# Mish feed-forward on one core: the first w1 loads split, tile 0 transposed k by k, and b1 moved to SP's queue

## The chip, the cores and the metric

The kernel runs on one core of one Trainium2 chip. A core has a matrix engine (TensorE, in the profile PE, with its weight loads as PEld), a vector engine (DVE), a scalar engine for activation functions (ACT), a general engine (POOL) and a fifth sequencer (SP) that mostly issues DMAs. All of them run side by side, each on its own list of instructions, and meet only at semaphores. Sixteen DMA engines move data between device memory (HBM) and the on-chip memory (SBUF). Matmul results land in eight banks of PSUM.

The metric is the device time of one execution in microseconds, the median of several runs. Less is better.

## The reference

x is 2048 x 512 (bf16), w1 is 512 x 1792, b1 has 1792 values, w2 is 1792 x 512. What must be computed:

```python
h   = jnp.einsum("bsd,df->bsf", x, w1) + b1
sp  = jnp.log1p(jnp.exp(-jnp.abs(h))) + jnp.where(h > 0, h, 0)
act = h * jnp.tanh(sp)            # mish
out = jnp.einsum("bsf,fd->bsd", act, w2)
```

So there are two products with an activation between them: 2048 x 512 x 1792 and 2048 x 1792 x 512.

## The kernel before

The rows of x are worked in four blocks of 512 rows. For each block the first product is made transposed: for each of the 14 column groups f of w1 (128 columns each) four matmuls over k (the 512 inner values in groups of 128) gather h for 128 columns x 512 rows in one PSUM bank (`mm1`). ScalarE then writes mish of it, with the bias, to SBUF (`mish`, L153). The second product goes by tiles of 128 rows: 14 matmuls over f into a bank (`mm2`), which VectorE copies out (`put`, L192) and SP stores.

The first product needs x transposed, with k along the partitions. For blocks 1 to 3 the DMA engines do that while they load (`DMA_TRANSPOSE`, the last three loads on SP's queue). Block 0 would come too late that way, so its four 128-row tiles are loaded as they are and transposed on TensorE by `transpose_x` (L133 to L148): per tile four 128 x 128 transposes (one for each k) into PSUM, and two copies to SBUF, each of two k: VectorE takes k 0 and 1, ScalarE k 2 and 3.

Everything is written out by hand, so each engine works in the order of the program. The loads are issued on two queues (L91 to L112):

- on ScalarE's queue: w1 k 0-1 and w1 k 2-3, each for the first four column groups (256 KB each), then b1;
- on SP's queue: x tile 0, x tile 1 (128 KB each), x tiles 2 and 3 together (256 KB), w1 for column groups 4 to 7, w1 for groups 8 to 13, all of w2, then the three transposing loads.

While the first loads are under way TensorE runs six dummy matmuls of 512 columns (`WARM`, `dummy`). Then, with `first(js, ks)` standing for the products of tiles js with w1 rows ks for the first four column groups, its order is (L204 to L230):

```python
transpose_x(0); transpose_x(1)
first((0,), (0, 1)); first((1,), (0, 1)); first((0, 1), (2,))
transpose_x(2); transpose_x(3)
first((0, 1), (3,)); first((2, 3), (0, 1))
# b1: copied into a padded tile, transposed on TensorE, copied to b1_sb
first((2, 3), (2, 3))
```

A product of one tile has 128 moving columns, one of two tiles 256. After this come the ten remaining column groups of block 0 with 512 columns each, the second product of block 0, and the other three blocks. A matmul waits for the w1 load that it reads (`t_w1`) and for the copies of its tiles (`t_cp`), a transpose for the load of its tile (`t_xn`) and for the copy that last read its PSUM bank (`free`).

Of the kernel before, what the change touches and what calls it, by code (L numbers as in the profile page):

```python
# [4 lines left out]

P = 128
WARM = (512,) * 6
BLOCKS = (512, 512, 512, 512)


# [21 lines left out]
def bass_standalone__dense_activation_mish__prompt_kernel(  # L32
# [10 lines left out]
    BF, F32 = dt.bfloat16, dt.float32  # L43
# [3 lines left out]
    KT, FT = D // P, F // P  # L47
# [5 lines left out]
    F0 = 4  # L53
    N0 = BLOCKS[0] // P

    with ExitStack() as es:
        def sb(name, shape, t):
            return es.enter_context(nc.sbuf_tensor(name, shape, t))

        x_nat = sb("x_nat", [P, N0, D], BF)  # L60
        xT = sb("xT", [P, KT, S], BF)
        w1_sb = sb("w1_sb", [P, KT, F], BF)
        w2_sb = sb("w2_sb", [P, FT, D], BF)
        b1_nat = sb("b1_nat", [FT, P], BF)
# [6 lines left out]
        ps = es.enter_context(nc.psum_tensor("ps", [P, 8, 512], F32))  # L71

        def sem(name):
            return es.enter_context(nc.semaphore(name))

        sp = Stream(nc.sync, None)
        pe = Stream(nc.tensor, sem("c_pe"))
        dve = Stream(nc.vector, sem("c_dve"))
        act = Stream(nc.scalar, sem("c_act"))
        pool = Stream(nc.gpsimd, sem("c_pool"))  # L80

        def load(q, dst, src, name, transpose=False):
            s = sem(name)
            (q.eng.dma_start_transpose if transpose else q.eng.dma_start)(dst, src).then_inc(s, 16)  # L84
            return (s, 16)

        def load_w1(q, ks, a, b):
            return load(q, w1_sb[:, ks, a * P:b * P], w1v[:, ks, a * P:b * P], "s_w1_%d_%d" % (ks.start, a))


        t_xn, t_w1, t_w2 = [None] * N0, {}, {}  # L91
        for ks in (slice(0, 2), slice(2, 4)):
            t = load_w1(act, ks, 0, F0)
            for f in range(F0):
                for k in range(ks.start, ks.stop):
                    t_w1[k, f] = t
        for j in range(2):
            t_xn[j] = load(sp, x_nat[:, j, :], x2[j * P:(j + 1) * P, :], "s_xn%d" % j)
        t_xn[2] = t_xn[3] = load(sp, x_nat[:, 2:4, :], x2[2 * P:4 * P, :].rearrange("(j p) d -> p j d", p=P), "s_xn2")
        t_b1 = load(act, b1_nat[:, :], b1.rearrange("(j p) -> j p", p=P), "s_b1")  # L100
        for a, b in ((4, 8), (8, FT)):
            t = load_w1(sp, slice(0, KT), a, b)
            for f in range(a, b):
                for k in range(KT):
                    t_w1[k, f] = t
        t = load(sp, w2_sb[:, :, :], w2v, "s_w2")
        for f in range(FT):
            t_w2[f] = t
# [16 lines left out]
        def dummy(n):  # L125
            nc.tensor.matmul(ps[:, 7, 0:n], c_w, c_m[:, 0:n], start=True, stop=True)  # L126


        free = [[] for _ in range(8)]
        t_cp = {}  # L130
        t_mish = {}

        def transpose_x(j):  # L133

            pe.wait(t_xn[j], t_id)
            for h, eng in ((0, dve), (1, act)):
                bank = 2 * (j % 2) + h
                pe.wait(*free[bank])
                psb = ps[:, bank, 0:P].bitcast(BF)
                for i in range(2):  # L140
                    k = 2 * h + i
                    mm = nc.tensor.transpose(psb[:, i * P:(i + 1) * P], x_nat[:, j, k * P:(k + 1) * P], ident[:, :])  # L142
                eng.wait(pe.mark(mm))
                dst = xT[:, 2 * h:2 * h + 2, j * P:(j + 1) * P]
                src = psb.rearrange("p (k t) -> p k t", k=2)
                t = eng.mark(nc.vector.tensor_copy(dst, src) if eng is dve else act.eng.activation(dst, src, ACT.Copy))  # L146
                t_cp[j, h] = t
                free[bank] = [t]  # L148

        def mish(s, f, bank, t_mm):  # L150
            n = BLOCKS[s]
            act.wait(t_b1c, t_mm)
            t = act.mark(act.eng.activation(a_sb[:, f, starts[s]:starts[s + 1]], ps[:, bank, 0:n], ACT.Mish,  # L153
                                            bias=b1_sb[:, f:f + 1]))
            t_mish[s, f] = t
            free[bank] = [t]

        def mm1_step(s, f, k, bank, js=None):

            n = BLOCKS[s]  # L160
            lo, hi = (0, n) if js is None else (js[0] * P, (js[-1] + 1) * P)
            first = k == 0 and lo == 0
            if first:
                pe.wait(*free[bank])
            pe.wait(t_w1[k, f])
            if s:
                pe.wait(t_xT[s])
            else:
                pe.wait(*[t_cp[j, k // 2] for j in (js or range(N0))])
            return nc.tensor.matmul(ps[:, bank, lo:hi], w1_sb[:, k, f * P:(f + 1) * P],  # L170
                                    xT[:, k, starts[s] + lo:starts[s] + hi], start=first, stop=(k == KT - 1 and hi == n))

        def mm1(s, f, bank):
            for k in range(KT):
                mm = mm1_step(s, f, k, bank)
            mish(s, f, bank, pe.mark(mm))
# [24 lines left out]
            put(i, lo, hi, bank, pe.mark(mm))  # L201


        for n in WARM:  # L204
            dummy(n)
# [12 lines left out]
        transpose_x(2)  # L218
        transpose_x(3)
        dve.wait(t_b1, t_bz)  # L220
        t_b1p = dve.mark(nc.vector.tensor_copy(b1_pad[0:FT, :], b1_nat[:, :]))  # L221
        first((0, 1), (3,))
        first((2, 3), (0, 1))
        pe.wait(t_b1p, *free[0])
        psb1 = ps[:, 0, 0:P // 2].bitcast(BF)
# [3 lines left out]
        free[0] = [t_b1c]  # L229
# [44 lines left out]
```

## Time and profile before

| | |
|---|---|
| median of 3 runs | 105.64 us (105.47 to 106.13) |
| the profiled execution: its own time | 105.42 us |
| the profiled execution: its span, first to last instruction | 104.2 us |
| PE busy | 100.7 us (97%) |
| ACT busy | 40.3 us (39%) |
| DVE busy | 12.7 us (12%) |
| granted clock of TensorE, mean | 1.000 |

The profile is one execution. Its page gives busy times by engine, the chain of work that ended last (followed back from the last instruction, each step to what released it), groups of instructions by line, and DMA issues with the time from issue to landing. Other views of the same trace show instructions in order of time, the waits, one tile's or line's instructions, and the packets of each DMA queue in a stretch. Times in them are microseconds from the start of the span, and "mean" durations of matmuls contain the time that a result takes through the array, so that matmuls that follow each other overlap. q1 is SP's DMA queue, q10 ScalarE's.

### The profile page before, as it was taken

To read this page: it belongs to the slowest core of one execution; us is meant where nothing else is said; L and a number is where in the kernel's file an instruction comes from. 1 tells how busy PE (TensorE), PEld (TensorE's weight loads), DVE (VectorE), ACT (ScalarE), POOL (GpSimd) and SP (SyncE) were. 2 spreads that over 40 slices of the span, in tenths; PEclk is the share of its full clock that TensorE was granted. 3 is DMA by queue.
4 is the path that set the end of the run, shared out by engine and by line. 5 is a ranking of instruction groups with operands and counts; after the bars stand their busy time and mean duration, and the time that the engine had idled before them with its cause. 6 is when DMAs were issued, how large, how long until landed. Compare 5 with 4: busy or idle time off the path is not lost.

```text
span 104.2 us, 1154 instructions
## 1 busy us (share of the span) xinstructions
PE 100.7 (97%) x500; PEld 48.1 (46%) x509; DVE 12.7 (12%) x24; ACT 40.3 (39%) x61; POOL 0.7 (1%) x6
## 2 busy tenths in 40 slices
PE   6899999999999999999999999999999999999992
PEld 2576444444444444444444444444444444444462
DVE  0220000022220000022220000022112000011223
ACT  0726987000027777200007777500005777700000
POOL 2000000000000000000000000000000000000000
DMA  1999998961101000010111000001111000001111
GB/s 62 343 318 377 350 219 185 257 163 50 37 13 50 0 0 6 0 47 3 50 50 50 0 3 0 0 6 50 50 50 50 0 0 0 0 6 50 50 50 50
DMA packets 12689, 7.94 MB, mean 76 GB/s; under 512 B 6796, under 2 KB 12684, under 8 KB 12684
## 3 DMA queue, kind: packets, MB, share of 16 engines
q1 hardware_dynamic: 12112, 7.34, 25.8%
q10 hardware_dynamic: 572, 0.53, 1.6%
q8 instruction: 4, 0.07, 0.2%
q14 instruction: 1, 0.01, 0.0%
HBM read 4.20 MB, written 2.10 MB: 60 GB/s over the span
## 4 chain that ended last, share of the span: by engine, by line
PE 94%; DMA 3%; issue 1%; SPq 0%; DVE 0%
PE ps L170 46%; PE ps L186 46%; DMA x_nat<-in_x_dram 3%; PE ps L142 1%; SPq L84 0%; DVE o_sb L192 0%; PE ps L226 0%
## 5 line engine op out<-in xcount | busy, mean ns | idle before, releaser
L153 ACT ACTIVATE a_sb<-ps,b_sb 128x512 bf16<-128x512 f32 x56 | 37.6, 691 | 46.1 <-PE ps L170 46.0
L170 PE MATMUL ps<-xT,w_sb 128*128 128x512 bf16 (+2 forms) x243 | 49.1, 358 | 0.3
L186 PE MATMUL ps<-w_sb,a_sb 128*128 128x512 bf16 (+2 forms) x234 | 48.8, 366 | 0.2
L170 PEld LDWEIGHTS ps<-xT,w_sb 128*128 128x128 bf16 x248 | 23.4, 98 | 24.7 <-DVE b_pad L221 0.2
L186 PEld LDWEIGHTS ps<-w_sb,a_sb 128*128 128x128 bf16 x238 | 22.8, 98 | 25.9
L192 DVE CAST o_sb<-ps 128x512 bf16<-128x512 f32 (+2 forms) x17 | 11.2, 660 | 83.0 <-PE ps L186 83.0
L126 PE MATMUL ps<-const-bfloat16-1.0 128*128 128x512 bf16 x6 | 2.7, 623 | 0.8 <-PEq L259 0.8
L120 ACT ACT_TABLE_LOAD x1 | 1.3, 1283 | 2.5 <-issue 2.5
L146 ACT ACTIVATE xT<-ps 128x256 bf16<-128x256 bf16 x4 | 1.4, 382 | 1.9 <-PE ps L142 1.9
L142 PE MATMUL ps<-ident,x_nat 128*128 128x128 bf16 x16 | 1.8, 256 | 0.3 <-DMA x_nat<-in_x_dram 0.3
L142 PEld LDWEIGHTS ps<-ident,x_nat 128*128 128x128 bf16 x16 | 1.2, 115 | 1.4 <-DMA x_nat<-in_x_dram 1.4
L146 DVE COPY xT<-ps 128x256 bf16<-128x256 bf16 x4 | 1.1, 292 | 4.8 <-PE ps L142 4.8
L126 PEld LDWEIGHTS ps<-const-bfloat16-1.0 128*128 128x128 bf16 x6 | 0.7, 133 | 1.9 <-issue 1.9
L228 DVE CAST b_sb<-ps 128x14 f32<-128x14 bf16 x1 | 0.2, 173 | 1.2 <-PE ps L226 1.2
L118 POOL TENSOR_SCALAR_AFFINE_SELECT ident<-ones 128x128 bf16<-128x128 bf16 x1 | 0.3, 294 | 0.1
L115 DVE MEMSET b_pad<- 128x64 uint32 x1 | 0.1, 112 | 0.9 <-PEq L259 0.9
L226 PE MATMUL ps<-ident,b_pad 128*128 128x128 bf16 x1 | 0.2, 219 | 0.0
L116 POOL MEMSET ones<- 128x128 bf16 x1 | 0.2, 205 | 0.3 <-POOLq L259 0.3
L221 DVE COPY b_pad<-b_nat 14x128 bf16<-14x128 bf16 x1 | 0.2, 173 | 0.0
L226 PEld LDWEIGHTS ps<-ident,b_pad 128*128 128x128 bf16 x1 | 0.1, 98 | 0.0
L259 POOL MEMSET const-bfloat16-1.0<- 128x1 bf16 x1 | 0.1, 103 | 0.0
L259 POOL MEMSET const-uint8-127<- 128x1 uint8 x1 | 0.1, 103 | 0.0
(2 smaller groups left out, 0.2 us busy)
## 6 DMA issues: line engine op xcount, KB each, us to landing
out_dram<-o_sb SPq DMA_DIRECT2D x15, 128.0 KB, 1.7
w_sb<-in_w_dram SPq DMA_DIRECT2D x1, 1792.0 KB, 13.6
w_sb<-in_w_dram SPq DMA_DIRECT2D x1, 768.0 KB, 7.7
w_sb<-in_w_dram ACTq DMA_DIRECT2D x2, 256.0 KB, 3.6
w_sb<-in_w_dram SPq DMA_DIRECT2D x1, 512.0 KB, 6.1
x_nat<-in_x_dram SPq DMA_DIRECT2D x2, 128.0 KB, 2.7
x_nat<-in_x_dram SPq DMA_DIRECT2D x1, 256.0 KB, 4.3
out_dram<-o_sb SPq DMA_DIRECT2D x1, 96.0 KB, 1.6
```

The costliest lines, as they stand in the source:

```text
L116: t_ones = pool.mark(pool.eng.memset(ones[:, :], 1.0))
L118: t_id = pool.mark(pool.eng.affine_select(ident[:, :], ones[:, :], pattern=[[1, P]], compare_op=ALU.is_equal, fill=0.0, base=0, channel_mu ...
L120: act.eng.preload_act_table(ACT.Mish)
L126: nc.tensor.matmul(ps[:, 7, 0:n], c_w, c_m[:, 0:n], start=True, stop=True)
L142: mm = nc.tensor.transpose(psb[:, i * P:(i + 1) * P], x_nat[:, j, k * P:(k + 1) * P], ident[:, :])
L146: t = eng.mark(nc.vector.tensor_copy(dst, src) if eng is dve else act.eng.activation(dst, src, ACT.Copy))
L153: t = act.mark(act.eng.activation(a_sb[:, f, starts[s]:starts[s + 1]], ps[:, bank, 0:n], ACT.Mish, bias=b1_sb[:, f:f + 1]))
L170: return nc.tensor.matmul(ps[:, bank, lo:hi], w1_sb[:, k, f * P:(f + 1) * P], xT[:, k, starts[s] + lo:starts[s] + hi], start=first, stop=( ...
L186: return nc.tensor.matmul(ps[:, bank, 0:hi - lo], a_sb[:, f, i * P:(i + 1) * P], w2_sb[:, f, lo:hi], start=(f == 0), stop=(f == FT - 1))
L192: t = dve.mark(nc.vector.tensor_copy(o_sb[:, i, lo:hi], ps[:, bank, 0:hi - lo]))
L221: t_b1p = dve.mark(nc.vector.tensor_copy(b1_pad[0:FT, :], b1_nat[:, :]))
L226: t_b1t = pe.mark(nc.tensor.transpose(psb1, b1_pad[:, :], ident[:, :]))
```

## The change

Five things are changed, all in the first microseconds:

- the first loads of w1 on ScalarE's queue are three and not two: k 0 (128 KB), k 1 (128 KB), k 2-3 (256 KB);
- b1 is no longer the third load on ScalarE's queue, but the fourth on SP's, ahead of w1 for groups 4 to 7;
- `transpose_x` takes a list of banks. Tile 0 uses four, one for each k, with four copies of one k each (VectorE k 0 and 2, ScalarE k 1 and 3). The other tiles use two, as before, with other bank numbers;
- tile 0's products with k 0 stand ahead of tile 1's transposes, its products with k 1 behind them;
- the sixth dummy matmul has 256 columns instead of 512, and one more of 256 columns stands between tile 0's transposes and its first products.

A product of block 0 now waits for the copy of its own k.

```diff
-WARM = (512,) * 6
+WARM = (512,) * 5 + (256,)
...
-        for ks in (slice(0, 2), slice(2, 4)):
-            t = load_w1(act, ks, 0, F0)
...
+        for k0, k1 in ((0, 1), (1, 2), (2, 4)):
+            load_part(act, k0, k1, 0, F0)
...
-        t_b1 = load(act, b1_nat[:, :], b1.rearrange("(j p) -> j p", p=P), "s_b1")
...
+        t_b1 = load(sp, b1_nat[:, :], b1.rearrange("(j p) -> j p", p=P), "s_b1")
+        load_part(sp, 0, KT, 4, 8)
+        load_part(sp, 0, KT, 8, FT)
...
-        def transpose_x(j):
+        def transpose_x(j, banks):
 
             pe.wait(t_xn[j], t_id)
-            for h, eng in ((0, dve), (1, act)):
-                bank = 2 * (j % 2) + h
+            n = KT // len(banks)
+            for h, bank in enumerate(banks):
+                eng = (dve, act)[h % 2]
                 pe.wait(*free[bank])
-                psb = ps[:, bank, 0:P].bitcast(BF)
-                for i in range(2):
-                    k = 2 * h + i
+                psb = ps[:, bank, 0:n * P // 2].bitcast(BF)
+                for i in range(n):
+                    k = n * h + i
...
-                t_cp[j, h] = t
+                for i in range(n):
+                    t_cp[j, n * h + i] = t
...
-                pe.wait(*[t_cp[j, k // 2] for j in (js or range(N0))])
+                pe.wait(*[t_cp[j, k] for j in (js or range(N0))])
...
-        transpose_x(0)
-        transpose_x(1)
-        first((0,), (0, 1))
+        transpose_x(0, (0, 1, 2, 3))
+        dummy(256)
+        first((0,), (0,))
+        transpose_x(1, (0, 1))
+        first((0,), (1,))
         first((1,), (0, 1))
         first((0, 1), (2,))
-        transpose_x(2)
-        transpose_x(3)
+        transpose_x(2, (2, 3))
+        transpose_x(3, (0, 1))
```

b1's transpose uses bank 2 instead of bank 0. `load_part` is the old loop over `load_w1` with its tokens, made a function.

More of the change, by code (lines that the diff above doesn't have):

```diff
@@ L91, in bass_standalone__dense_activation_mish__prompt_kernel, with load_part @@
         t_xn, t_w1, t_w2 = [None] * N0, {}, {}
-        for ks in (slice(0, 2), slice(2, 4)):
-            t = load_w1(act, ks, 0, F0)
-            for f in range(F0):
-                for k in range(ks.start, ks.stop):
+        def load_part(q, k0, k1, a, b):
+            t = load_w1(q, slice(k0, k1), a, b)
+            for f in range(a, b):
+                for k in range(k0, k1):
                     t_w1[k, f] = t
+        for k0, k1 in ((0, 1), (1, 2), (2, 4)):
+            load_part(act, k0, k1, 0, F0)
         for j in range(2):
@@ L99, in bass_standalone__dense_activation_mish__prompt_kernel @@
         t_xn[2] = t_xn[3] = load(sp, x_nat[:, 2:4, :], x2[2 * P:4 * P, :].rearrange("(j p) d -> p j d", p=P), "s_xn2")
-        t_b1 = load(act, b1_nat[:, :], b1.rearrange("(j p) -> j p", p=P), "s_b1")
[L101 to L105, printed above, removed]
+        t_b1 = load(sp, b1_nat[:, :], b1.rearrange("(j p) -> j p", p=P), "s_b1")
+        load_part(sp, 0, KT, 4, 8)
+        load_part(sp, 0, KT, 8, FT)
         t = load(sp, w2_sb[:, :, :], w2v, "s_w2")
@@ L131, in bass_standalone__dense_activation_mish__prompt_kernel @@
         t_mish = {}
-        def transpose_x(j):
+        def transpose_x(j, banks):
             pe.wait(t_xn[j], t_id)
-            for h, eng in ((0, dve), (1, act)):
-                bank = 2 * (j % 2) + h
+            n = KT // len(banks)
+            for h, bank in enumerate(banks):
+                eng = (dve, act)[h % 2]
                 pe.wait(*free[bank])
-                psb = ps[:, bank, 0:P].bitcast(BF)
-                for i in range(2):
-                    k = 2 * h + i
+                psb = ps[:, bank, 0:n * P // 2].bitcast(BF)
+                for i in range(n):
+                    k = n * h + i
                     mm = nc.tensor.transpose(psb[:, i * P:(i + 1) * P], x_nat[:, j, k * P:(k + 1) * P], ident[:, :])
                 eng.wait(pe.mark(mm))
-                dst = xT[:, 2 * h:2 * h + 2, j * P:(j + 1) * P]
-                src = psb.rearrange("p (k t) -> p k t", k=2)
+                dst = xT[:, n * h:n * h + n, j * P:(j + 1) * P]
+                src = psb.rearrange("p (k t) -> p k t", k=n)
                 t = eng.mark(nc.vector.tensor_copy(dst, src) if eng is dve else act.eng.activation(dst, src, ACT.Copy))
-                t_cp[j, h] = t
+                for i in range(n):
+                    t_cp[j, n * h + i] = t
                 free[bank] = [t]
@@ L201, in mm2 @@
             put(i, lo, hi, bank, pe.mark(mm))
-        for n in WARM:
-            dummy(n)
-        transpose_x(0)
-        transpose_x(1)
         def first(js, ks):
@@ L213, in first @@
                         mish(0, f, 4 + f, pe.mark(mm))
-        first((0,), (0, 1))
+        for n in WARM:
+            dummy(n)
+        transpose_x(0, (0, 1, 2, 3))
[3 more added lines that the diff above has]
+        first((0,), (1,))
         first((1,), (0, 1))
         first((0, 1), (2,))
-        transpose_x(2)
-        transpose_x(3)
+        transpose_x(2, (2, 3))
+        transpose_x(3, (0, 1))
         dve.wait(t_b1, t_bz)
@@ L223, in bass_standalone__dense_activation_mish__prompt_kernel @@
         first((2, 3), (0, 1))
-        pe.wait(t_b1p, *free[0])
-        psb1 = ps[:, 0, 0:P // 2].bitcast(BF)
+        pe.wait(t_b1p, *free[2])
+        psb1 = ps[:, 2, 0:P // 2].bitcast(BF)
         t_b1t = pe.mark(nc.tensor.transpose(psb1, b1_pad[:, :], ident[:, :]))
@@ L228, in bass_standalone__dense_activation_mish__prompt_kernel @@
         t_b1c = dve.mark(nc.vector.tensor_copy(b1_sb[:, :], psb1[:, 0:FT]))
-        free[0] = [t_b1c]
+        free[2] = [t_b1c]
         first((2, 3), (2, 3))
```

## The prediction

> **What bounds the kernel now.** I read the page first, for the engine that fills the span, and then the chain of work that ended last, in order of time, for the places where that engine is held up.
>
> ```profile
> span 104.2 us, 1154 instructions
> PE 100.7 (97%) x500; PEld 48.1 (46%) x509; DVE 12.7 (12%) x24; ACT 40.3 (39%) x61; POOL 0.7 (1%) x6
> PE 94%; DMA 3%; issue 1%; SPq 0%; DVE 0%
> ```
> ```profile
> 1.27 2.93 DMA x_nat<-in_x_dram
> 4.20 0.05 issue
> 4.25 0.51 PE ps L142 x4
> ...
> 6.11 0.62 PE ps L142 x8
> ...
> 9.11 8.58 PE ps L170 x39
> ```
>
> TensorE (PE) is the bound for 94% of the chain. The only link that is not PE work and is longer than 0.1 us at the front is the load of x tile 1, which lands at 1.27 + 2.93 = 4.20. From 6.11 on the chain is PE without a gap that the change touches. So whatever the change does before the transposes of tiles 2 and 3 (6.11) counts only as far as it moves that 6.11; what comes behind it is the same list of matmuls. The sum is therefore: **when do the transposes of tiles 2 and 3 start in the changed kernel, less 6.11**. What leads up to it stands in the timeline of the first microseconds (start, length, instruction, idle before it):
>
> ```profile
> 0.84 2.72 PE L126 MATMUL ps<-const-bfloat16-1.0 128*128 128x512 bf16 x6 [0.84 <-PEq L259]
> 3.26 0.45 PEld L142 LDWEIGHTS ps<-ident,x_nat 128*128 128x128 bf16 x4 [0.61 <-DMA x_nat<-in_x_dram]
> 3.35 0.63 PE L142 MATMUL ps<-ident,x_nat 128*128 128x128 bf16 x4
> 3.81 0.29 DVE L146 COPY xT<-ps 128x256 bf16<-128x256 bf16 x1 [2.81 <-PE ps L142]
> 4.25 0.51 PE L142 MATMUL ps<-ident,x_nat 128*128 128x128 bf16 x4 [0.27 <-DMA x_nat<-in_x_dram]
> 4.59 1.49 PE L170 MATMUL ps<-xT,w_sb 128*128 128x128 bf16 x20
> 6.10 0.45 PEld L142 LDWEIGHTS ps<-ident,x_nat 128*128 128x128 bf16 x8 [0.30 <-DMA x_nat<-in_x_dram]
> 6.11 0.62 PE L142 MATMUL ps<-ident,x_nat 128*128 128x128 bf16 x8
> 6.86 0.17 DVE L221 COPY b_pad<-b_nat 14x128 bf16<-14x128 bf16 x1
> ```
> ```profile
> 2.93 0.63 PE L126 MATMUL ps<-const-bfloat16-1.0 128*128 128x512 bf16 x1
> ```
> ```profile
> 5.82 0.27 PE L170 MATMUL ps<-xT,w_sb 128*128 128x256 bf16 x1
> ```
>
> Two readings. First, **the gap that the change fills**: PE is idle 0.27 us before 4.25, waiting for x tile 1. Second, **what is late next**: at 6.10 the weight loader has already waited 0.30 us for the load of x tiles 2 and 3. The last k 2 product starts at 5.82 and takes its 0.11 us of the array, so PE has nothing left from 5.93 on. The transposes at 6.11 start when that load lands.
>
> The clock can be read from the same rows. Four transposes take 0.63 us at 3.35 and eight take 0.62 at 6.11. With a last one of 0.31 and 0.22 us (the extremes of the row below) the spacing is 0.107 and 0.057 us. The four at 4.25 take 0.51, between the two (four would take 0.63 and 0.39), so the clock doubles during them, at about 4.5.
>
> ```profile
> L142 PE MATMUL ps<-ident,x_nat x16: 219/225/314, 3.4 to 6.5; 128*128 128x128 bf16 x16
> L84 SPq DMA_DIRECT2D x_nat<-in_x_dram x3: 397/407/427, 0.8 to 1.7; - x3
> ...
> DMA to landing us min/median/max: 2.4/2.9/4.3
> ```
> ```profile
> L84 ACTq DMA_DIRECT2D w_sb<-in_w_dram x2: 462/474/487, 0.8 to 1.3; - x2
> L84 ACTq DMA_DIRECT2D b_nat<-in_b_dram x1: 707/707/707, 1.8 to 1.8; - x1
> ...
> DMA to landing us min/median/max: 3.1/3.6/4.1
> ```
>
> From these: x tile 0 lands at 0.8 + 2.4 = 3.2, x tiles 2 and 3 at 1.7 + 4.3 = 6.0 to 6.1, w1 k 0-1 at 0.8 + 3.1 = 3.9, w1 k 2-3 at 1.3 + 4.1 = 5.4.
>
> **The change part by part.** *PE's order.* The dummies lose half of one: the sixth started at 2.93, five starts in 2.09 us give 0.42 each, half is 0.21, so they end at 3.14 and not 3.35. Tile 0's transposes then start when x tile 0 is there: 3.28. Four at 0.107: to 3.71. The new dummy, 0.21: to 3.92. Meanwhile the k 0 copy: first transpose out at 3.28 + 0.31, VectorE starts 0.04 later (as at 3.81), and half the columns cost between 0.17 (the L221 row) and 0.29; done by 3.80 to 3.92, under the dummy. Four k 0 products at the low clock, 0.107 each: to 4.35. Tile 1's transposes, two at 0.107, two at 0.057: to 4.68, where before they were done at 4.59. Four k 1 products: to 4.91. Here the new order **adds a wait**: tile 1's first products need VectorE's copy, which starts at 4.46 + 0.31 + 0.04 = 4.81, takes 0.29, and is seen 0.05 later (the issue row behind x tile 1's landing): 5.15. Before, eight products covered that copy, now four do; 0.24 us of idle, queued behind it everything PE has. Eight products: to 5.60. Four k 2 products at 0.109: to 6.04. So from PE's side alone the transposes of tiles 2 and 3 could start at 6.04, **0.07 earlier** than 6.11, and no better: the filled 0.27 us goes into the dummy, the low clock of the k 0 products and the thinner cover of tile 1's copy.
>
> *The copies.* ScalarE and VectorE get one more copy each (0.17 to 0.38 us), both early, when they have nothing else; PE waits for no other of them. The bank numbers change, but each bank's previous copy is done long before. Cost nothing; if the k 1 copy on ScalarE held tile 1's second bank, 0.1 at most.
>
> *The loads.* This is where I see the sum decided. The packets by queue (q1 is SP's, q10 ScalarE's), in the stretches 2.7 to 3.15, 4.05 to 4.5 and 4.5 to 4.95:
>
> ```profile
> q10 hardware_dynamic: 151, 0.15, 96.3%
> q1 hardware_dynamic: 12, 0.01, 7.2%
> ```
> ```profile
> q10 hardware_dynamic: 136, 0.13, 82.7%
> q1 hardware_dynamic: 39, 0.04, 28.4%
> ```
> ```profile
> q1 hardware_dynamic: 143, 0.15, 92.6%
> q10 hardware_dynamic: 32, 0.01, 11.6%
> ```
>
> The two queues do not share: the loads go one after the other, x 0, w1 k 0-1 (2.7), x 1, w1 k 2-3 (4.05), x 2-3 (4.5), in the order in which their issues ended. In the first stretch x 1 had been issued since 1.67 and still moved only 12 packets. With three w1 loads the list becomes x 0, k 0, x 1, k 1 and then a pair of 256 KB loads, w1 k 2-3 and x 2-3, whose order is open. x 2-3 is issued third on SP, done at 1.7 + 0.43 = 2.15 as now. w1 k 2-3 is now third on ScalarE too: 0.80 plus two issues of 0.40 (SP's one-block row) to 0.46 (ScalarE's two-block row), 0.03 between them, plus its own 0.46 to 0.49: done at 2.12 to 2.27. Most of that lies behind 2.15. I take **x 2-3 first**. Then they swap places: the same bytes lie ahead of the second one as now, so w1 k 2-3 lands where x 2-3 landed, at 6.06, and not at 5.4. But PE's order asks for it first: the k 2 products stand ahead of the transposes of tiles 2 and 3. They start at 6.11, take 4 x 0.109 = 0.44, and the transposes start at 6.55. **Sum: +0.44 us.** Bounds: 5.6 for the landing (PE is not ready earlier) gives -0.07; 6.3 gives +0.7.
>
> The Trainium skill, "DMA: Bandwidth & Descriptors", section "Queues, rings and completion order", has each DMA engine take turns between its queues, packet by packet. By that rule the pair would interleave and both would land near 6.06, whichever was issued first, for the same +0.44; the 151 against 12 packets above do not show such turns.
>
> *b1 on SP's queue.* Its issue (0.71) stands ahead of the two w1 loads, w2 and the transposing loads there; they are issued that much later, from 2.9 instead of 2.19.
>
> ```profile
> w_sb<-in_w_dram SPq DMA_DIRECT2D x1, 1792.0 KB, 13.6
> w_sb<-in_w_dram SPq DMA_DIRECT2D x1, 512.0 KB, 6.1
> ```
> ```profile
> 2.19 1.57 SPq L84 DMA_DIRECT2D w_sb<-in_w_dram  x3
> ...
> 17.31 4.63 PEld L186 LDWEIGHTS ps<-w_sb,a_sb 128*128 128x128 bf16 x22
> ```
>
> What hides it is the backlog: SP's packets for w1 columns 4-8 come after x 2-3, near 5, long after 2.9 + 0.5. They land at 2.19 + 6.1 = 8.3, with 0.8 us to the first use at 9.11. w2 lands at 3.25 + 13.6 = 16.85 (third of the three issues, 0.5 each), 0.46 us ahead of its first weights at 17.31. If the full 0.71 came through, w2 would cost 0.25; with PE 0.44 later itself, nothing. b1 lands behind x 2-3 and is wanted by VectorE at 6.86 or later. I take zero for all of it. On ScalarE's side the table load comes earlier, which nothing waits for.
>
> **Rivals.**
>
> *A, w1 k 2-3 first.* For it: ScalarE's first issue started as early as SP's, and if a one-block issue costs it 0.40 it is done at 2.12, ahead by 0.03. Then 5.4 and 6.06 stay as they are, the wait for x 2-3 takes the place of the one for x 1, and the transposes start at 6.04 to 6.11; if k 0 also goes ahead of x 0, x 0 comes up to 0.45 later and they start near 6.25. -0.07 to +0.15: 105.35 to 105.57. This is also the case in which the change fills its gap and it brings nothing.
>
> *C, the clock comes one window later.* Place: between the shortened dummies (idle 3.14 to 3.28) and 4.5. If PE then runs at the low clock up to 7.9, tile 1's transposes end at 4.78, k 1 at 5.21, tile 1's products at 6.06, k 2 (0.21 each) at 6.96, the eight transposes at 7.82 instead of 6.56: +1.26, 106.7, **slower by over 1%**. It decides if the doubling comes after about 7.2. Against it: the new order has PE busier between 3.7 and 4.6 than the old one. The Trainium skill, "TensorE: Matmul & The Clock Gate", Part 1, gives a free-running window of about 3.4 us of activity after which the clock doubles, varying from run to run; this trace agrees in size (0.84 to about 4.5), and cannot show the variation.
>
> *D, w2 or the w1 columns late*, by the shift of SP's issues: up to +0.3 beside the others.
>
> **How the numbers follow.** The profiled execution took 105.42 us (104.2 of span, 1.2 around it); the median of the runs shown is 105.64, 0.22 above. The likeliest, x 2-3 first: 105.42 + 0.44 = 105.86 on the profiled one, 106.08 on the median. I give 105.95, between. Chances: this 0.52 (+0.2 to +0.7), A 0.36, C 0.06, D alone 0.04, 0.02 for something faster that I don't see. Range: from A on the lower footing less 0.15 for scatter (the runs of before span 0.66), 105.2, to +0.7 on the upper footing and C's start, 106.7. A measurement of this kernel can tell about 1%, 1.06 us, from no change; only C is beyond it, with a little of D on top of the likeliest: slower 0.08, same 0.90, faster 0.02.
>
> **What would show it.** Right: in the timeline the four 256-wide k 2 products start at about 6.1, after a wait of the weight loader on the w1 load of some 0.5 us, and the eight transposes at about 6.55 without a wait on x. Traffic by queue: q1 ahead of q10 from about 3.7. Wrong: eight transposes at 6.1 after a wait on x (A), or 128-wide products 0.107 apart behind 5 (C); a wait on w1 or w2 ahead of L173's 512-wide or L189's first matmul (D). The prediction fails most easily on the order of two issues that I place 0.1 us apart.

## The result and the profile after

The changed kernel takes 107.05 us (median of 4 runs, 106.75 to 107.47), the kernel before on the same chip 105.88 us: a ratio of 1.0104, with a 95% interval of 1.0059 to 1.0149. The change costs 1.2 us. The forecast was 105.95 with a range of 105.2 to 106.7; it had the sign right and the size wrong. The profiled execution took 107.12 us, 1.70 more than that of before (105.42). Slow executions, over 1.5% above the fastest of their kernel, are left out of all ratios and of the medians of the experiments.

The page of the changed kernel, its span and the shares of the chain of work that ended last, and then that chain in order of time (start, length, what):

```profile
span 105.9 us, 1167 instructions
...
PE 91%; DMA 5%; ACTq 1%; DVE 0%; issue 0%
```
```profile
1.73 5.59 DMA w_sb<-in_w_dram
7.32 0.04 issue
7.37 0.61 PE ps L173 x4
7.98 0.45 PE ps L144 x8
8.42 1.40 PE ps L173 x12
```

Where the chain of before had the load of x tile 1 (2.93 us, ending at 4.20), it now has one load of w1: issued at 1.73, landed at 7.32. It is w1 k 2-3. The timeline shows the place where PE stands for it (rows of the dummies, the copies and the DMA issues are left out):

```profile
3.46 0.34 PEld L144 LDWEIGHTS ps<-ident,x_nat 128*128 128x128 bf16 x4 [0.81 <-DMA x_nat<-in_x_dram]
4.16 0.59 PE L173 MATMUL ps<-xT,w_sb 128*128 128x128 bf16 x4
4.54 0.63 PE L144 MATMUL ps<-ident,x_nat 128*128 128x128 bf16 x4
4.96 1.49 PE L173 MATMUL ps<-xT,w_sb 128*128 128x128 bf16 x12
7.36 0.33 PEld L173 LDWEIGHTS ps<-xT,w_sb 128*128 128x128 bf16 x4 [1.18 <-DMA w_sb<-in_w_dram]
7.37 0.61 PE L173 MATMUL ps<-xT,w_sb 128*128 128x256 bf16 x4 [0.92 <-DMA w_sb<-in_w_dram]
7.81 0.61 PE L144 MATMUL ps<-ident,x_nat 128*128 128x128 bf16 x8
```

The gap ahead of tile 1's transposes is filled, as the change says: they follow tile 0's k 0 products at 4.54 without a wait, though 0.29 us later than the 4.25 of before. Then the weight loader waits 1.18 us for w1, the four k 2 products start at 7.37, and the eight transposes of tiles 2 and 3 start at 7.81, without a wait on x. Before they started at 6.11: 1.70 us later, and 107.12 is 1.70 above 105.42. Nothing was lost or won behind that point.

Why the load is so late stands in the stretches of the front part (from:to, length, busy us of PE, PEld, DVE, ACT and POOL with counts, granted clock, share of the DMA engines, GB/s). The clock column reads 1.00 in all of them, also where the spacing of the products, 0.107 us and not 0.057, shows the low clock; so in this document the clock is read from the spacing. The kernel before:

```profile
2.50:3.75 1.25, 1.25 (x7) 0.60 (x5) 0.00 (x0) 1.21 (x1) 0.00 (x0) 1.00 1.08 341
3.75:5.00 1.25, 0.98 (x15) 0.76 (x12) 0.58 (x2) 0.67 (x3) 0.00 (x0) 1.00 1.03 347
5.00:6.25 1.25, 1.23 (x19) 0.93 (x17) 0.00 (x0) 0.18 (x1) 0.00 (x0) 1.00 0.89 244
```

The changed kernel:

```profile
2.50:3.75 1.25, 1.13 (x6) 0.44 (x5) 0.00 (x0) 1.00 (x1) 0.00 (x0) 1.00 1.08 348
3.75:5.00 1.25, 1.25 (x13) 1.03 (x12) 0.45 (x3) 0.49 (x2) 0.00 (x0) 1.00 0.67 118
5.00:6.25 1.25, 1.25 (x14) 1.17 (x12) 0.29 (x1) 0.38 (x1) 0.00 (x0) 1.00 0.95 326
```

The last number is the reading. Between 2.5 and 3.75 the two move the same. Then the traffic of the changed kernel **falls to a third, 118 GB/s for 1.25 us**, where before it was 347. This stretch is called the trough below. The share of the DMA engines falls less, to 0.67, so they are partly idle and partly held by packets that take long: the 45 packets between 3.75 and 4.2 filled 65% of the sixteen engines' time, 104 ns each, where the 175 of before between 4.05 and 4.5 filled 111%, 46 ns each.

The missing 229 GB/s over 1.25 us are 286 KB, but the next stretch makes up 103 KB of them. What the trough is worth at the landing shows in the bytes that the two queues had moved: in the kernel before up to 6.06, when x 2-3 landed, then in the changed kernel up to 6.65 and up to 7.32, when w1 k 2-3 landed:

```profile
DMA packets 1317, 1.24 MB, mean 205 GB/s; under 512 B 108, under 2 KB 1317, under 8 KB 1317
...
DMA packets 1333, 1.24 MB, mean 187 GB/s; under 512 B 124, under 2 KB 1333, under 8 KB 1333
...
DMA packets 1572, 1.49 MB, mean 203 GB/s; under 512 B 129, under 2 KB 1572, under 8 KB 1572
```

The changed kernel has moved the 1.24 MB of before at 6.65, **0.59 us later: that is the slower flow**. The other 0.67 of the 1.26 us between 6.06 and 7.32 lie behind the load's own last packet. From 6.6 to 7.37 the packets by queue have one row, SP's, and none of ScalarE's:

```profile
q1 hardware_dynamic: 273, 0.28, 109.1%
```

So the last packet of w1 k 2-3 had started by 6.6, and PE was told of the load **0.7 us after that**, while later loads moved on at full rate. In the kernel before this took about 0.3 us for x 2-3: sixteen packets of 4 bytes close each load, and the last of x 2-3's starts at 5.75. Why the end takes longer is open.

The order in which the loads share the queues is new too. Packets by queue between 2.7 and 3.15 (q1 SP, q10 ScalarE), in the changed kernel:

```profile
q1 hardware_dynamic: 108, 0.10, 61.8%
q10 hardware_dynamic: 81, 0.07, 44.0%
```

Before there were 12 and 151 in this stretch. With x 0 and k 0 of one size the two queues run side by side in it; before, w1 k 0-1 ran nearly alone. All nineteen profiles of this case agree: where the first loads of the two queues are of one size (ten kernels), q1 moved 58 to 112 packets here and q10 44 to 90; where w1's is twice x tile 0's (nine kernels), 2 to 30 and 135 to 166. In the changed kernel x tile 0 lands later, and its transposes start at 3.46 and not at 3.35.

### The profile page after: what moved, and what is told of

The parts are those of the page before. It is cut to its first block, busy times and chain, and to the rows that moved or that the text cites. A ratio compares the mean times of both kernels' runs of the same rounds, so it can differ in the third digit from the quotient of the medians.

```text
span 105.9 us, 1167 instructions
## 1 busy us (share of the span) xinstructions
PE 102.2 (97%) x510; PEld 49.0 (46%) x510; DVE 12.8 (12%) x25; ACT 40.4 (38%) x62; POOL 0.7 (1%) x6
## 4 chain that ended last, share of the span: by engine, by line
PE 91%; DMA 5%; ACTq 1%; DVE 0%; issue 0%
PE ps L189 46%; PE ps L173 45%; DMA w_sb<-in_w_dram 5%; ACTq L84 1%; PE ps L144 0%; DVE o_sb L195 0%; PE ps L231 0%
## 5 line engine op out<-in xcount | busy, mean ns | idle before, releaser
L173 PE MATMUL ps<-xT,w_sb 128*128 128x512 bf16 (+2 forms) x248 | 50.6, 364 | 0.9 <-DMA w_sb<-in_w_dram 0.9
L173 PEld LDWEIGHTS ps<-xT,w_sb 128*128 128x128 bf16 x248 | 24.1, 100 | 26.1 <-DMA w_sb<-in_w_dram 1.2
L127 PE MATMUL ps<-const-bfloat16-1.0 128*128 128x512 bf16 (+1 forms) x7 | 2.9, 564 | 0.8 <-PEq L264 0.8
L148 ACT ACTIVATE xT<-ps 128x256 bf16<-128x256 bf16 (+1 forms) x5 | 1.5, 340 | 3.9 <-PE ps L144 3.9
L148 DVE COPY xT<-ps 128x256 bf16<-128x256 bf16 (+1 forms) x5 | 1.2, 265 | 6.4 <-PE ps L144 6.4
```

## The experiments

The first theory (P) was that the two 256 KB loads, x 2-3 and w1 k 2-3, disturb each other because both are now issued at 1.73. Its rival (S) was b1 on SP's queue, the one other change among the loads. Times are medians; ratios are to the kernel before, run on the same chips. The traffic in the two stretches of interest, 3.75 to 5.0 and 5.0 to 6.25, is gathered in a table behind the experiments.

**b1 back on ScalarE's queue.**

```diff
-        t_b1 = load(sp, b1_nat[:, :], ...)
+        t_b1 = load(act, b1_nat[:, :], ...)
```

> The changed kernel with b1 back on ScalarE's queue, now as its fourth load. Theory P (pair): the trough in the traffic between 3.75 and 5.0 us comes from w1 k 2-3 and x 2-3, two 256 KB loads that are issued in the same moment on the two queues; b1 has no part. Then w1 k 2-3 lands near 7.3 again, the transposes of tiles 2 and 3 start near 7.8, and the time is that of the changed kernel, 106.8 to 107.4 us. Theory S (small load): b1's 14 short rows on SP's queue hold back the descriptors around them. Then the trough is gone, w1 k 2-3 lands near 6.1, the transposes start near 6.55, and the time is near 106.0 to 106.3 us.

Measured: 107.81 us, 1.0203 (1.0156 to 1.0249). S falls. But P's number is missed too: this is slower than the changed kernel, beyond both intervals, and w1 k 2-3 landed at 8.0, although the trough is softer (203 and then 306 GB/s, where the changed kernel had 118 and 326). The packets by queue between 6.25 and 8.0 show what went on:

```profile
DMA packets 535, 0.60 MB, mean 341 GB/s; under 512 B 31, under 2 KB 535, under 8 KB 535
...
q1 hardware_dynamic: 487, 0.56, 95.9%
q10 hardware_dynamic: 48, 0.03, 6.6%
```

The traffic is back, but it is SP's: 0.56 MB, more than twice the size of x 2-3, while ScalarE's queue, with the load that PE waits for, moved 0.03. So a low traffic is not the whole of the delay: later loads pass the one that PE waits for. Why b1's place matters here, and not in the next run, is open.

**The kernel before with b1 on SP's queue, and nothing else.**

> The kernel before with one edit alone: b1 fourth on SP's queue. Theory P: w1 k 2-3 lands at 5.4 and x 2-3 at 6.1 as before, the transposes start at 6.1, no difference in time (105.5 to 106.1 us). Theory S: a trough behind x 2-3's issue, the transposes of tiles 2 and 3 start 0.5 to 1.3 us later than 6.1, 106.2 to 107.2 us.

Measured: 105.79 us, 0.9995 (0.9962 to 1.0028): no difference. In the kernel before b1's move costs nothing, as the prediction had it.

**The changed kernel with w1's first loads as before.**

```diff
-        for k0, k1 in ((0, 1), (1, 2), (2, 4)):
+        for k0, k1 in ((0, 2), (2, 4)):
```

> The changed kernel with w1's first loads as before, k 0-1 and k 2-3, and all else of the change kept (order on PE, four banks, dummies, b1 on SP). Theory P: w1 k 2-3 is issued at 1.3 again, ahead of x 2-3; it lands near 5.4, x 2-3 near 6.1, no trough, and the time is that of the kernel before within 0.3 us. Theory S: the trough stays, w1 k 2-3 or x 2-3 lands near 7, 106.6 us or more. If the order on PE or its clock costs by itself, the transposes start later than the load of x 2-3 lets them, by 0.1 to 0.6 us.

Measured: 105.52 us, 0.9977 (0.9947 to 1.0007). **The whole loss is gone with this one edit**, and the rest of the change is worth between -0.5% and +0.1%. Its timeline is the test of the prediction's sum for PE:

```profile
4.80 1.49 PE L173 MATMUL ps<-xT,w_sb 128*128 128x128 bf16 x16
6.13 0.61 PE L144 MATMUL ps<-ident,x_nat 128*128 128x128 bf16 x8
...
5.23 0.78 PEld L173 LDWEIGHTS ps<-xT,w_sb 128*128 128x128 bf16 x12 [0.22 <-DVE xT L148]
```

The added wait for VectorE's copy of tile 1 is there (0.22 us; 0.24 was said), and PE gets to the eight transposes at 6.13 (6.04 was said).

**w1 in four loads of 128 KB.**

```diff
+        for k0, k1 in ((0, 1), (1, 2), (2, 3), (3, 4)):
```

> The changed kernel with four w1 loads of 128 KB, k 0, k 1, k 2, k 3, so that no 256 KB load of w1 is issued beside x 2-3. Theory P, if the slow pair needs two 256 KB loads of two blocks each: the trough shrinks, k 2 lands by 6.0, and the time falls to 105.6 to 106.3 us. If any two loads that are issued in the same moment there do it: k 2 lands near 6.5 and the time lies between, 106.3 to 107.0. Theory S: as the changed kernel, 106.8 to 107.4 us.

Measured: 106.42 us, 1.0067 (1.0044 to 1.0089): between, as P's second form said. But the next two runs are against P.

**b1 third on SP's queue, so that x 2-3 is issued half a microsecond behind w1 k 2-3.**

```diff
+        t_b1 = load(sp, b1_nat[:, :], ...)
         t_xn[2] = t_xn[3] = load(sp, x_nat[:, 2:4, :], ...)
-        t_b1 = load(sp, b1_nat[:, :], ...)
```

> The changed kernel with one issue moved: b1 third on SP's queue, so that x 2-3 is issued near 2.25 and not at 1.73, half a microsecond behind w1 k 2-3 (1.73). The bytes, the sizes of the loads and x 0, k 0, x 1, k 1 in pairs stay. Theory P (the trough comes from the two 256 KB loads issued in the same moment): the trough between 3.75 and 5.0 is gone, w1 k 2-3 lands near 5.4 and x 2-3 near 6.1 to 6.4, the transposes start at 6.1 to 6.5, 105.5 to 106.2 us. Theory Q (it comes from the two queues having run in pairs from the start, whichever loads follow): the trough stays, w1 k 2-3 lands at 6.5 or later, 106.5 to 107.5 us.

Measured: 106.59 us, 1.0066 (1.0019 to 1.0114). x 2-3 was issued at 2.24, but w1 k 2-3 still landed only at 6.7. P's numbers are missed; Q's are met in the time and in the landing, with a softer trough (241 GB/s).

**w1 k 2-3 moved to SP's queue, behind x 2-3.**

```diff
+        for k0, k1 in ((0, 1), (1, 2)):
...
+        load_part(sp, 2, 4, 0, F0)
```

> The changed kernel with w1 k 2-3 moved from ScalarE's queue to SP's, right behind x 2-3: the same three sizes, but one queue alone carries both 256 KB loads. Theory P: no trough, x 2-3 lands near 5.4 and w1 k 2-3 near 6.1, the k 2 products start at 6.1 and the transposes at 6.55, 0.44 later than before: 105.9 to 106.4 us. This is the order of loads that the prediction took, without the trough. Theory Q: trough, both later than 6.5, 106.5 us or more.

Measured: 106.70 us, 1.0055 (1.0020 to 1.0089). The trough only moved: 302 GB/s in the first stretch, 162 in the second, and w1 k 2-3 landed at 7.3, again as Q said. That the two loads are issued in the same moment is not needed for it. P falls as the whole cause.

**The k 2 products behind the transposes of tiles 2 and 3, loads untouched.**

```diff
-        first((0, 1), (2,))
         transpose_x(2, (2, 3))
...
-        first((0, 1), (3,))
+        first((0, 1), (2, 3))
```

> The changed kernel with its loads untouched, and the k 2 products of tiles 0 and 1 moved behind the transposes of tiles 2 and 3, together with their k 3 products. If the time is set by w1 k 2-3 standing ahead of x 2-3 in PE's order: the transposes start when x 2-3 lands (6.9 in the changed kernel's profile) and are done when w1 k 2-3 lands (7.3), 0.45 us of PE work leaves the path, 106.5 to 106.7 us. If the low clock or the order of the first products set it, no difference from the changed kernel, 106.8 to 107.4 us.

Measured: 106.75 us, 1.0075 (1.0038 to 1.0113), against 1.0104 for the changed kernel. The direction is the expected one, but the intervals overlap. The profile shows the mechanism: PE now waits for x, not for w1, and the transposes come first.

```profile
7.17 0.62 PE L144 MATMUL ps<-ident,x_nat 128*128 128x128 bf16 x8 [1.27 <-DMA x_nat<-in_x_dram]
7.63 1.58 PE L173 MATMUL ps<-xT,w_sb 128*128 128x256 bf16 x13
```

**The kernel before with x 0 and x 1 as one load of 256 KB**, so that equal loads of 256 KB stand first on both queues.

```diff
+        t_xn[0] = t_xn[1] = load(sp, x_nat[:, 0:2, :], ...)
```

> The kernel before with x tiles 0 and 1 loaded as one load of 256 KB, so that SP's and ScalarE's queues issue two 256 KB loads in the same moment twice, at 0.8 and at 1.3, and nothing else is changed. Theory P: both pairs interleave and the traffic falls into a trough, in less than 250 GB/s over a stretch of more than 0.5 us between 2.5 and 5.0, where the kernel before moved 300 to 380; w1 k 2-3 or x 2-3 lands later than 6.5. Theory Q, or a cause of that one place: no trough, x 2-3 lands near 6.1. The first transposes start later in any case, near 3.9 to 4.3, since tile 0 waits for both tiles.

Measured, in one execution: 107.6 us, which says little, since tile 0 starts late and the clock stayed low to about 8.4. Its traffic: 228 GB/s between 2.5 and 3.75, then 380 and 371. Two 256 KB loads issued at 0.8 run slowly, the two issued at 1.3 do not. P would have had both slow; x 2-3 landed at 6.0, as Q said.

The next four asked whether it is the split of w1's first load, the number of loads (N) or the equal first loads (Q).

**The kernel before with w1 split as in the change, and nothing else.**

```diff
-        for ks in (slice(0, 2), slice(2, 4)):
+        for ks in (slice(0, 1), slice(1, 2), slice(2, 4)):
```

> The kernel before with one edit alone: w1's first loads as k 0, k 1, k 2-3. b1 stays on ScalarE's queue, PE's order, banks and dummies stay. If the split of the first w1 load is the whole cause: fewer than 1120 KB moved by 6.0 us (1201 in the kernel before, 989 in the changed one), w1 k 2-3 lands at 6.7 to 8.0, 106.4 to 107.9 us. If it needs PE's new order as well: 105.5 to 106.1 us.

Measured: 106.95 us, 1.0115 (1.0066 to 1.0164), from three executions between 106.21 and 107.56. The split alone gives a loss as large as the whole change's. The profiled execution is the fastest of them, and in it the trough is weak (279 and 308 GB/s) and w1 k 2-3 landed at 6.4, earlier than was said. With the run that takes the split out of the changed kernel, this closes the question which part of the change it is.

**The kernel before with the second w1 load split.**

```diff
+        for ks in (slice(0, 2), slice(2, 3), slice(3, 4)):
```

> The kernel before with the second w1 load split instead of the first: k 0-1, k 2, k 3. As many loads as in the changed kernel, but the first two on the queues stay unequal, 128 KB of x and 256 KB of w1. Theory Q (the first loads on the two queues are of one size and shape, their packets alternate from the start, and the later loads come late): no loss, 1150 KB or more by 6.0 us, 105.4 to 106.2 us. Theory N (each further load costs traffic, wherever it stands): below 1120 KB by 6.0, 106.4 us or more.

Measured: 106.13 us, 1.0050 (1.0023 to 1.0076), with a trough of 165 GB/s in the second stretch. Q, equal first loads as the whole cause, falls: here they are unequal. The loss is half of the changed kernel's.

**The kernel before with x 2 and x 3 as two loads on SP's queue.**

```diff
+        for j in range(4):
             t_xn[j] = load(sp, x_nat[:, j, :], ...)
```

> The kernel before with x tiles 2 and 3 as two loads of 128 KB. One more load on SP's queue, the first ones on both queues unchanged. Theory Q: no loss, 1150 KB or more by 6.0, and tile 2's transposes can start when its own load lands, near 5.7; 105.2 to 106.0 us. Theory N: below 1120 KB by 6.0, 106.2 us or more.

Measured: 105.69 us, 1.0011 (0.9974 to 1.0049). No trough: 358 and 335 GB/s, the best of all so far. N falls: a further load by itself, here on SP's queue, costs nothing.

**Another order: ScalarE k 0-1 and k 2; SP x 0, x 1, x 2-3, k 3, b1.** PE as in the changed kernel.

```diff
+        for k0, k1 in ((0, 2), (2, 3)):
...
+        load_part(sp, 3, 4, 0, F0)
```

> The changed kernel with other loads: ScalarE issues k 0-1 and k 2, SP issues x 0, x 1, x 2-3, then k 3, b1 and the rest. PE's order, banks and dummies as in the changed kernel. Theory Q: no trough; k 2 lands by 5.2, x 2-3 by 5.8, and PE's own work sets the start of the transposes at 6.0 to 6.15: 105.2 to 105.8 us, equal to the changed kernel with w1 in two loads (105.52), and at best 0.4% under the kernel before. Theory N: a trough, 106.2 us or more.

Measured: 105.32 us, 0.9976 (0.9952 to 1.0000); 360 and 264 GB/s. Two large loads on ScalarE's queue, and no loss.

What was left looked like ScalarE's queue (O): in each kernel with a trough but one, it had three loads of 128 KB or more. Three runs were made for that.

**x 3 third on ScalarE's queue, w1 untouched.**

```diff
+        t_xn[3] = load(act, x_nat[:, 3, :], x2[3 * P:4 * P, :], "s_xn3")
```

> The kernel before with x tiles 2 and 3 as two loads, and the second of them third on ScalarE's queue (the run with both on SP's queue moved 1330 KB by 6.0 us and lost nothing). Theory O (a third load of 128 KB or more on ScalarE's queue runs the DMA engines dry): the traffic between 3.75 and 6.25 falls below 280 GB/s, x tile 3 lands later than 6.4, 106.2 us or more. Theory H (it is the small loads of w1, whose 1 KB rows lie 3.5 KB apart in memory): no trough, 1250 KB or more by 6.0, 105.3 to 106.0 us.

Measured: 106.03 us, 1.0013 (0.9980 to 1.0047). The trough is there, 177 GB/s in the second stretch, without any split of w1; the time does not show it, and there O's number (106.2 or more) is missed. None of w1 is late here, and the two x tiles landed at 6.4 and 6.6. In the profiled execution PE, at the low clock, was not done with its products before 6.91, so it waited for neither; what the loads cost the faster executions it does not show. O holds for the traffic, and small w1 loads are not needed.

**The queues of the first loads exchanged.**

```diff
-            load_part(act, k0, k1, 0, F0)
+            load_part(sp, k0, k1, 0, F0)
...
-            t_xn[j] = load(sp, ...)
+            t_xn[j] = load(act, ...)
-        t_xn[2] = t_xn[3] = load(sp, ...)
+        t_xn[2] = t_xn[3] = load(act, ...)
```

> The changed kernel with the queues of the first loads exchanged: SP issues k 0, k 1, k 2-3, ScalarE issues x 0, x 1, x 2-3; the later loads stay on SP. Theory O: ScalarE's queue still has three loads, so the trough stays: under 200 GB/s in 3.75 to 5.0, 106.5 us or more; the same by theory H. If instead it matters that SP's queue is served first: w1 k 2-3 lands ahead of x 2-3 and the time falls below 106.2.

Measured: 106.77 us, 1.0065 (1.0044 to 1.0086), 212 GB/s in the first stretch: a trough again, softer than O and H said. w1 k 2-3, now SP's, landed ahead of x 2-3 (6.7 and 7.1), and that did not bring the time below 106.2.

**The w1 loads read from w2's rows.**

```diff
+            t = load(act, w1_sb[:, k0:k1, 0:F0 * P], w2v[:, k0:k1, :], ...)
```

> The changed kernel with its three w1 loads on ScalarE's queue reading the same number of bytes from w2, whose 1 KB rows follow each other in memory, in place of w1's first four column groups. Queues, sizes, shapes on chip and all work stay; h of these four column groups is computed from the wrong weights, and that alone is changed in the output. Theory H: the trough is gone or halved (250 GB/s or more in 3.75 to 5.0), w1 k 2-3's stand-in lands by 6.3, 105.6 to 106.4 us. Theory O, or a limit in how the loads are handed to the DMA engines: the trough stays, under 200 GB/s, 106.7 to 107.5 us.

Measured: 106.70 us, 1.0062 (1.0038 to 1.0085). 326 GB/s in the first stretch, as H said, but 235 in the second, and the load landed at 6.9, not by 6.3. Neither theory's numbers. The scattered rows may have a part; they are not the whole cause, since 0.6% of loss stays.

**Two loads for w1 and four for x, PE's new order**, and **the same with tile 1 copied k by k** (the last two lines, in the second run only).

```diff
+        for k0, k1 in ((0, 2), (2, 4)):
...
+        for j in range(4):
             t_xn[j] = load(sp, x_nat[:, j, :], ...)
...
-        transpose_x(1, (0, 1))
+        transpose_x(1, (0, 1, 2, 3))
```

> The changed kernel with w1 in two loads (k 0-1, k 2-3) as before and x tiles 2 and 3 as two loads on SP's queue; b1 on SP, and PE's order, banks and dummies of the changed kernel. Two loads of 128 KB or more on ScalarE's queue, four on SP's. If the rule that the runs left standing (two large loads on ScalarE's queue, and the first of them twice x tile 0's size) is right: no trough, 1250 KB or more by 6.0, tile 2's transposes start when PE is ready, near 6.0 to 6.1; 105.2 to 105.6 us, 0.1 to 0.5% below the kernel before. If not: below 280 GB/s between 3.75 and 6.25, 106.0 us or more.

> As the run beside it, and tile 1 too is transposed into four banks and copied k by k. If VectorE's copy of tile 1 holds PE (the prediction's added wait, 0.22 us in the changed kernel with two w1 loads): the first product of tile 1 starts 0.1 to 0.2 us earlier, and the time falls by at most that, 105.1 to 105.6 us. If the load of x tile 3 or the clock sets the start of the transposes instead, no difference between the two.

Measured: 105.39 us, 0.9970 (0.9943 to 0.9998), and 105.56 us, 0.9972 (0.9946 to 0.9998). Neither has a trough: 382 and 334 GB/s, 362 and 353. Both beat the kernel before by 0.3%, just beyond their intervals, and the changed kernel by 1.3%, by the quotient of the ratios (1.0104 to 0.9970 and 0.9972), which were taken on different chips. The copies k by k for tile 1 bring nothing that these runs can tell.

The table: large is 128 KB or more; the traffic in GB/s is that of the one profiled execution. The run with x 0 and x 1 as one load has no ratio and is not in it.

| kernel | large loads on ScalarE's queue | 3.75-5.0 | 5.0-6.25 | ratio |
|---|---|---|---|---|
| before | 2 | 347 | 244 | 1 |
| before, b1 on SP | 2 | 347 | 327 | 0.9995 |
| changed, w1 in two | 2 | 328 | 325 | 0.9977 |
| before, x in four | 2 | 358 | 335 | 1.0011 |
| third order | 2 | 360 | 264 | 0.9976 |
| x in four, new order | 2 | 382 | 334 | 0.9970 |
| the same, tile 1 k by k | 2 | 362 | 353 | 0.9972 |
| changed | 3 | 118 | 326 | 1.0104 |
| changed, b1 on ScalarE | 3 | 203 | 306 | 1.0203 |
| changed, w1 in four | 4 | 231 | 291 | 1.0067 |
| changed, b1 third | 3 | 241 | 261 | 1.0066 |
| changed, k 2 behind | 3 | 219 | 320 | 1.0075 |
| before, w1 in three | 3 | 279 | 308 | 1.0115 |
| before, k 2 and k 3 | 3 | 273 | 165 | 1.0050 |
| before, x 3 on ScalarE | 3 | 326 | 177 | 1.0013 |
| changed, queues exchanged | 3 | 212 | 306 | 1.0065 |
| changed, w2 as source | 3 | 326 | 235 | 1.0062 |
| changed, k 2-3 on SP | 2 | 302 | 162 | 1.0055 |

**What is settled:** the split of w1's first load makes the loss; taking it out of the change removes the loss, and putting it alone into the kernel before gives all of it. It does so by a late load: in the changed kernel PE stands for w1 k 2-3.

**What the table does not show** is that the traffic alone makes the load late. Added up over both columns, the traffic does not tell the size of the loss: 503 GB/s go with 1.0013 (x 3 on ScalarE), 509 with 1.0203 (b1 on ScalarE) and 587 with 1.0115 (w1 in three).

The two last versions were built by the rule of at most two large loads on ScalarE's queue, the first of them larger than x 0, and they moved as much as it says. That is no hard test, since their early loads are those of "before, x in four", which had no trough, but for b1's place.

**What stays open** is why the traffic falls, why a load's end takes longer, and why later loads can pass the one that PE waits for. The last row has a trough with two large loads, and there the first loads on both queues are equal. "Three large ones on ScalarE's queue, or equal first loads" fits every row, but it was read off these rows afterwards; it is no cause.

## Why the prediction was wrong

*The frame held.* "When do the transposes of tiles 2 and 3 start in the changed kernel, less 6.11" gives 7.81 - 6.11 = 1.70, and the profiled executions differ by 1.70. It holds in all the profiles: in seventeen of the nineteen the time is the start of these transposes plus 99.3 us (99.29 to 99.37); the two others are the run with the k 2 products behind them (99.66) and the one whose clock was still low there (99.52). On the medians it is 1.2, since the profiled execution of before, at 105.42, lies 0.46 below the median of 105.88 and that of the changed kernel 0.07 above its own.

*The order of the landings held.* Both third loads were issued at 1.73, and the issues of the two queues ended at 2.16 (SP, 0.81 + 1.35) and 2.19 (ScalarE, 0.80 + 1.39): the order that the prediction took came true by 0.03 us. x 2-3 landed at 1.7 + 5.2 = 6.9 and w1 k 2-3 at 1.73 + 5.6 = 7.3, so PE's k 2 products waited for the later one. That wait was the forecast's mechanism. The issue rows of the changed kernel:

```profile
w_sb<-in_w_dram ACTq DMA_DIRECT2D x2, 128.0 KB, 2.9
x_nat<-in_x_dram SPq DMA_DIRECT2D x2, 128.0 KB, 2.7
x_nat<-in_x_dram SPq DMA_DIRECT2D x1, 256.0 KB, 5.2
w_sb<-in_w_dram ACTq DMA_DIRECT2D x1, 256.0 KB, 5.6
```

*The step that failed* is this one: "the same bytes lie ahead of the second one as now, so w1 k 2-3 lands where x 2-3 landed, at 6.06". It took the traffic of before for granted and changed only the order. The load came at 7.32, 1.26 later, and 0.44 + 1.26 is the 1.70. Much the same bytes did lie ahead of it, but they took longer: the 1.24 MB that before had moved by 6.06 were reached at 6.65, 0.59 us late. The other 0.67 us lie between the load's last packet and its landing, a time that the prediction took over from x 2-3 (about 0.3 us) and that was 0.7 here. The upper bound, "6.3 gives +0.7", was no bound either: it let the landing slip by a quarter of a microsecond, and nothing in it stood for a slower flow. A row of before could have warned: 244 GB/s between 5.0 and 6.25, at a time when loads were queued. At that rate the 434 KB of the 1.25 us from 3.75 on (347 GB/s) take 0.53 us longer, which puts the landing at 6.6; that bound too would have been 0.7 us short.

*The sentence under it* was "The two queues do not share". It was too strong for the kernel before itself: between 3.15 and 3.6, a stretch that the prediction does not show, q1 moved 103 packets and q10 72. In the changed kernel they stand 108 to 81 already in the stretch where before had 12 to 151. The rule that the Trainium skill gives in "DMA: Bandwidth & Descriptors", section "Queues, rings and completion order", that a DMA engine turns between the queues packet by packet, agrees with this row, though counts over 0.45 us do not show single turns; the prediction had set it aside on the 151 to 12 of before. By that rule it had both loads near 6.06, and they landed at 6.9 and 7.3, so the rule alone would not have saved the sum.

*PE's own sum* was right where it could be seen alone: 6.04 forecast, 6.13 measured with w1 in two loads. In the changed kernel's profile it was not: the twelve 128-wide products took 1.49 us from 4.96, the time of sixteen in the other run, four of them twice as wide, because the clock was still low (the last six took 0.84 us, 0.11 apart). That is rival C, in part. It cost nothing there, since PE waited for w1 anyway.

*b1 and what stands behind it on SP's queue* cost nothing in the kernel before, as said (0.9995). *The cases*: the result lies at the border of the 1% that the chances were cut at, at 1.04%. On the medians its 1.17 us lie between the likeliest case's +0.44 and C's +1.26, on the profiles its 1.70 lie above both; it came about by neither. (C's own sum is 0.06 too large: four k 2 products of 0.21 from 6.06 on end at 6.90 and not at 6.96.) The chance of 0.08 for slower by over 1% was too small because the prediction saw only the clock as a way there.

## What to carry to other kernels

Where a stage is fed by loads that follow each other without slack, the split of one load can change the flow of all that follow, and not only their order. Here the bound for its cost needed two terms that the prediction did not have: a stretch at a low traffic (0.59 us), and a longer time from the awaited load's last packet to its landing (most of the other 0.67 us). Filling a wait of PE is worth only the distance to the next late load, which stands in the same timeline a few lines below. And a test of two edits, the suspect taken out of the change and the suspect alone put into the kernel before, told more than any comparison of the traces.

## What the runs showed of the hardware

Two things were not expected, beside the packets that run side by side where the first loads are equal. The first is the trough itself: with a third large load early on ScalarE's queue the DMA engines moved 118 to 279 GB/s in one of the two stretches, in all ten kernels. The kernel before has a dip of its own (244), so one stretch doesn't part the two kinds; both columns added do, though only just, and from one execution of each: 438 to 587 for these ten, 591 to 716 for the seven with two such loads and a larger first one.

The second is how much the moment at which TensorE's clock doubles differs between executions of nearly one kernel. The two last versions, each in its profiled execution, the same sixteen products (twelve of 128 columns, four of 256) and then the eight transposes. The first:

```profile
4.88 2.20 PE L172 MATMUL ps<-xT,w_sb 128*128 128x128 bf16 x16
6.92 0.61 PE L143 MATMUL ps<-ident,x_nat 128*128 128x128 bf16 x8
```

The second:

```profile
4.56 1.43 PE L172 MATMUL ps<-xT,w_sb 128*128 128x128 bf16 x16
5.82 0.64 PE L143 MATMUL ps<-ident,x_nat 128*128 128x128 bf16 x8
```

The sixteen are worth twenty of 128 columns, which at the low clock's 0.107 us each are 2.14 us and at 0.057 are 1.14; so the first kept the low clock to about 6.8, and the second had the high one. It had it from about 4: its four k 0 products at 3.94 took 0.40 us, where four at the low clock take 0.59 to 0.61. That makes 1.1 us between the starts of the transposes, and 106.21 against 105.19 us for the two executions. Their medians differ by 0.17 and the other way, and the twelve executions of the first kernel alone lie between 105.20 and 106.21. So a single profiled execution of this kernel carries about 1 us of chance, in these two profiles from the clock. The Trainium skill describes in "TensorE: Matmul & The Clock Gate", Part 1, a free-running window, so that the number of matmuls at the low clock differs from run to run; the two profiles agree with that in kind, and 1 us is its size here.
